# Seven quarter-size products in place of eight for half of a first layer, with float16 operands and partial sums seeded into PSUM by a copy

## The chip, the cores and the metric

The kernel runs on one core of a Trainium2 chip. The metric is device time in microseconds (us), as the median of several executions; the kernel before takes 293.1 us in the runs made for this study. A run more than 1.5% above the fastest of the same kernel counts as slow and is left out of the ratios. "Granted clock" is the share of full speed that the chip granted TensorE, as the trace records it.

## The reference

Sliding-window attention (window of 32 on each side, 8 heads of 64) is followed by two dense layers with a gelu between them:

```python
def _attn_ref(q, k, v):                       # q, k, v: (8, 8, 576, 64)
    scores = scale * np.matmul(q, k.transpose(0, 1, 3, 2))
    scores = np.where(np.abs(pos[:, None] - pos[None, :]) <= 32, scores, -1e9)
    ...                                       # softmax
    return np.matmul(attn, v)

def _moe_ref(x, w_in, w_out):                 # x: 4608 x 512, w_in: 512 x 2048, w_out: 2048 x 512
    h = x @ w_in
    g = h * (1.0 / (1.0 + np.exp(-1.702 * h)))
    return g @ w_out
```

## The kernel before

The 4608 rows are 36 *units* of 128 rows. The main loop goes by *windows* of two units (a and b, 256 rows). In window w the kernel computes attention of its own two units, the first layer of the pair before, and the second layer of the pair before that. The second layer already is a seven-product scheme (P1 to P7), whose operand sums VectorE makes (`g_sums`). The first layer is plain: eight groups of eight matmuls, each group followed by one gelu on ScalarE, in two PSUM banks by turns.

```python
    def two_banks(self, name, dtype=F32):
        return self.ps.tile([128, 2, 512 if dtype == F32 else 1024], dtype, name=name, tag="a", bufs=2)

    def layer1(self, t, d, kind="h"):
        ...
        hps = self.bank(kind, [128, 2, 256], F32, "h_ps")        # kind "h": two buffers
        ffs = (d, d + 8) if t > 2 else (2 * d, 2 * d + 1)
        for i in range(2):
            ff = ffs[i]
            for kr in range(self.NK):                            # NK = 4
                nc.tensor.matmul(hps[:, i, :], self.w_in_sb[:, kr, ff * 128:(ff + 1) * 128], self.xT[t][:, kr, :],
                                 start=(i == 0 and kr == 0), stop=(i == 1 and kr == self.NK - 1))
        nc.scalar.activation(self.g[t][:, ffs[0]:ffs[1] + 1:ffs[1] - ffs[0], :], hps, AF.Gelu_apprx_sigmoid)

    def window(self, w):                 # the steady part; t = w - 2; l1 holds the 8 groups of pair w - 1
        ...
        self.scores(a)
        self.scores(b)
        self.g_sums(t, 1, (0, 1))
        self.product(t, 1, "o")
        self.keep(t, 1, dve)
        self.product(t, 2, "h")
        self.g_sums(t, 1, (2, 3))
        ...                              # P5, softmax of a, P6, softmax of b
        run(l1)
        self.values(a)
        self.values(b)
        self.norm(a)
        self.x_T(a)
        self.product(t, 7)
        self.keep(t, 7, dve)
        self.result(t, 22)
        run(l1, 1)
        self.product(t, 4)
        self.result(t, 21, act)
        self.norm(b)
        self.x_T(b)
        self.product(t, 3)
        self.result(t, 12)
        run(l1, len(l1) - 4)
        self.g_sums(w - 1, 0)
        self.feed(w)                     # among other things four copies of v ("vo<-ve") on VectorE
        run(l1, 4)
```

The softmax here doesn't subtract the row's maximum and nothing guards it: scores larger than these inputs give would overflow.

Of the kernel before, what the change touches and what calls it, by code (L numbers as in the profile page):

```python
# [22 lines left out]
JT = 4  # L23
# [4 lines left out]
class _Kernel:  # L28
# [7 lines left out]
    def __init__(self, ctx, tc, q, k, v, w_in, w_out, out):  # L36
        self.tc, self.nc = tc, tc.nc
        self.q, self.k, self.v, self.w_in, self.w_out, self.out = q, k, v, w_in, w_out, out
        self.B, self.H, self.S, self.D = q.shape
        self.N = self.B * self.S  # L40
        self.DM = self.H * self.D
        self.DFF = w_in.shape[1]
        self.NK = self.DM // 128
        self.NFF = self.DFF // 128
        self.scale = 1.0 / (self.D ** 0.5)
        self.NU = self.N // 128
        self.NW = self.NU // 2

        def pool(name, bufs, **kw):
            return ctx.enter_context(tc.tile_pool(name=name, bufs=bufs, **kw))  # L50

        self.cst = pool("cst", 1)
        self.work = pool("work", 2)
        self.ps = pool("ps", 1, space=bass.MemoryType.PSUM)
        self.stage, self.paired = {}, set()
        self.span = {"A": (0, 320)}
        self.xT, self.g, self.o_ps = {}, {}, {}
        self.p, self.acc, self.x, self.sc = {}, {}, {}, {}
        self.gs, self.part, self.o_sb = {}, {}, {}

# [10 lines left out]
    def two_banks(self, name, dtype=F32):  # L71
        return self.ps.tile([128, 2, 512 if dtype == F32 else 1024], dtype, name=name, tag="a", bufs=2)


    def setup(self):
# [3 lines left out]
        self.w_in_sb = cst.tile([128, self.NK, self.DFF], BF16, name="w_in_sb")  # L79
# [141 lines left out]
    def load_raw(self, c, hp, eng):  # L221

        lo, size = self.tokens("A")
        raw = self.stage[c, "raw", hp] = self.cst.tile([size // JT, 2, JT * self.D], F32, name=f"{c}_raw{hp}")
        src = {"q": self.q, "k": self.k}[c]
        eng.dma_start(raw, src[0, 2 * hp:2 * hp + 2, lo:lo + size, :].rearrange("h (p j) d -> p h (j d)", j=JT))
# [30 lines left out]
    def score_banks(self):  # L257
        return self.two_banks("sc").rearrange("k e (h s) -> k e h s", s=SQ)
# [9 lines left out]
    def scores(self, u):  # L268
        nc = self.nc
        seen = u not in self.sc  # L270
        if seen:
            self.sc[u] = self.score_banks()
# [27 lines left out]
    def values(self, u, kinds=None):  # L300
        nc, D = self.nc, self.D
        p = self.p.pop(u)
        if kinds is None:
            both = self.two_banks("pv")[:, :, :4 * (D + 1)].rearrange("q i (h d) -> q i h d", d=D + 1)
# [11 lines left out]
    def norm(self, u):  # L316
        nc, D = self.nc, self.D
        acc = self.acc.pop(u)
        x = self.work.tile([128, self.H, D], BF16, name="x", tag="x", bufs=4)
# [14 lines left out]
    def x_T(self, u, kind=None, eng=None):  # L334
        nc = self.nc
        t, s = divmod(u, 2)
        if s == 0:
            self.xT[t] = self.work.tile([128, self.NK, 256], BF16, name="xT", tag="xT", bufs=4)
# [5 lines left out]
        tp = self.bank(kind, [128, 4, 128], BF16, "tp")  # L344
        for c in range(4):
            nc.tensor.transpose(tp[:, c, :], x[:, 2 * c:2 * c + 2, :], self.ident)  # L346
# [16 lines left out]
    def layer2(self, u, quarter, kind="o", eng=None):  # L363
# [9 lines left out]
        if quarter == 3:  # L373
            o_sb = self.work.tile([128, self.DM], F32, name="o_sb", tag="o_sb", bufs=4)
# [53 lines left out]
    def result(self, t, n, eng=None):  # L428
# [3 lines left out]
        if u not in self.o_sb:  # L432
            self.o_sb[u] = self.work.tile([128, self.DM], F32, name="o_sb", tag="o_sb", bufs=4)
# [33 lines left out]
    def head(self):  # L467
# [8 lines left out]
        self.setup_neg()  # L476
        for m in range(2):
            self.load_v(m)
# [138 lines left out]

    def window(self, w):
# [19 lines left out]
        if w == 4:  # L638
# [22 lines left out]
            loads()  # L661
            for m in (10, 11):
# [9 lines left out]
        self.scores(a)  # L672
        if w > 5:
            self.scores(b)
# [4 lines left out]
        if w == 5:  # L679
            self.scores(b)  # L680
# [9 lines left out]
        self.values(a)  # L690
        self.values(b)
# [4 lines left out]
        self.result(t, 22)  # L696
        run(l1, 1)
# [114 lines left out]
```

## Time and profile before

| what | before |
|---|---|
| time | 293.29 us (292.95 to 293.41, 3 runs); 293.12 in the rounds with the changed kernel |
| TensorE busy | 283.5 us, 97% of the span, granted clock 1.0 |
| VectorE, ScalarE, GpSimd busy | 62%, 62%, 35% |
| one window | 14.63 us, of which TensorE is busy 14.63 |

The lines behind this table, and how they are read, are in the prediction below. Two more are wanted later. The first is from the page's part on the chain that ended last (each engine's share of the chain of work that sets the end); the second is the page's row of the first sum of g (after the bar: busy us, mean ns of one; then the idle time before them).

```profile
PE 82%; DMA 12%; POOL 3%; DVE 1%; issue 1%; ACT 0%; POOLq 0%; DVEq 0%
...
L398 DVE TENSOR_TENSOR gs<-g 128x512 f16<-128x512 f16 x30 | 12.8, 425 | 38.3 <-ACT g L361 38.3
```

ScalarE has 0% of the chain and VectorE 1%. A sum of g takes 0.425 us. VectorE's idle time before these sums, 38.3 us, is spent waiting for gelus, and since VectorE is hardly on the chain, it costs next to nothing.

### The profile page before, as it was taken

Reading aid. Unit: us, or ns where it says so; the run is one execution under the profiler, and the core shown is the slowest. Engines: PE = TensorE matmul, PEld = TensorE weight load, DVE = VectorE, ACT = ScalarE, POOL = GpSimd, SP = SyncE. Lnnn points to the kernel's source line nnn. Section 1 sums busy time; section 2 is a strip of 40 time slices with the busy share of each in tenths; the row PEclk is TensorE's granted clock in tenths of the full one; section 3 lists DMA queues with packets and bytes.
Section 4 is the critical chain, followed back from the end, with each engine's and each line's share of the span. In section 5 each row is a group of like instructions: output and inputs, shape, how many; then the busy total and the mean of one; then the engine's idle time right before and its main releaser. Section 6 shows DMA issues by size and latency. Waiting matters only on the chain.

```text
span 291.9 us, 8879 instructions
## 1 busy us (share of the span) xinstructions
PE 283.5 (97%) x3759; PEld 234.3 (80%) x3759; DVE 181.9 (62%) x465; ACT 181.1 (62%) x265; POOL 102.2 (35%) x140
## 2 busy tenths in 40 slices
PE   7989998999999999999999999999999999999994
PEld 2668654866888888888888888888888888888883
DVE  6761556578566767676767675757575757573352
ACT  4576365695757676767676666666666666664330
POOL 8864424988536341642525343422000000000000
PEclk9999999999999999999999999999999999999999
DMA  9999998999999999999999999999925221212012
GB/s 150 188 199 205 198 184 136 171 132 133 187 138 173 147 190 140 176 135 159 160 188 107 168 122 141 146 149 138 166 42 146 39 90 20 93 20 90 2 72 73
DMA packets 144823, 38.78 MB, mean 133 GB/s; under 512 B 129936, under 2 KB 140432, under 8 KB 144784
## 3 DMA queue, kind: packets, MB, share of 16 engines
q0 software_dynamic: 97232, 18.16, 85.0%
q1 hardware_dynamic: 47104, 19.67, 39.3%
q8 instruction: 29, 0.48, 0.7%
q10 hardware_dynamic: 448, 0.39, 0.5%
q14 instruction: 10, 0.08, 0.1%
HBM read 36.96 MB, written 9.44 MB: 159 GB/s over the span
## 4 chain that ended last, share of the span: by engine, by line
PE 82%; DMA 12%; POOL 3%; DVE 1%; issue 1%; ACT 0%; POOLq 0%; DVEq 0%
PE h_ps L359 38%; PE o_ps L421 32%; DMA ks<-in_k_dram 5%; DMA ve<-in_v_dram 4%; PE pv L313 4%; PE o_ps L371 4%; PE sc L282 3%; DMA w_in_sb<-in_moe_w_in_dram 3%; POOL ve L168 1%; PE tp L187 1%; POOL ks L146 0%; POOL ks L206 0%; POOL qs L206 0%; PE tp L346 0%; DVE o_sb L439 0%
## 5 line engine op out<-in xcount | busy, mean ns | idle before, releaser
L359 PE MATMUL h_ps<-xT,w_in_sb 128*128 128x256 bf16 x1152 | 134.9, 273 | 0.0
L361 ACT ACTIVATE g<-h_ps 128x512 f16<-128x512 f32 x144 | 85.7, 596 | 75.8 <-PE h_ps L359 74.5
L359 PEld LDWEIGHTS <-w_in_sb 128*128 128x128 bf16 x1152 | 112.2, 98 | 13.4
L168 POOL DMA_DIRECT2D ve<-in_v_dram x41 | 34.4, 847 | 73.1 <-DVE rec L323 46.3
L421 PEld LDWEIGHTS <-gs 128*128 128x128 f16 x480 | 45.7, 98 | 6.0 <-issue 0.2
L421 PE MATMUL o_ps<-w_sum,gs 128*128 128x256 f16 x360 | 44.4, 273 | 0.0
L421 PEld LDWEIGHTS <-g 128*128 128x128 f16 x360 | 34.2, 98 | 4.5 <-ACT g L361 0.2
L288 ACT ACTIVATE p<-sc 128x1024 bf16<-128x1024 f32 x36 | 34.9, 1021 | 4.5 <-PE sc L282 4.4
L398 DVE TENSOR_TENSOR gs<-g 128x512 f16<-128x512 f16 x30 | 12.8, 425 | 38.3 <-ACT g L361 38.3
L114 DVE COPY part<-o_ps 128x256 f32<-128x256 f32 x45 | 19.1, 424 | 19.3 <-PE o_ps L421 18.2
L421 PE MATMUL o_ps<-w_out_sb,g 128*128 128x256 f16 x240 | 29.0, 273 | 0.0
L439 DVE TENSOR_TENSOR o_sb<-o_ps,part 128x256 f32<-128x256 f32 x45 | 19.0, 423 | 15.4 <-PE o_ps L421 14.7
L114 DVE COPY vo<-ve 64x528 bf16<-64x528 bf16 x71 | 23.8, 335 | 6.9 <-DMA ve<-in_v_dram 5.3
L156 POOL DMA_DIRECT2D qs<-in_q_dram x27 | 22.9, 869 | 7.2 <-DMA ks<-in_k_dram 6.0
L156 POOL DMA_DIRECT2D ks<-in_k_dram x27 | 22.8, 860 | 5.2 <-DMA ve<-in_v_dram 3.6
L324 DVE TENSOR_TENSOR x<-pv,rec 128x512 bf16<-128x512 f32 x33 | 22.8, 692 | 1.1
L371 PE MATMUL o_ps<-w_out_sb,g 128*128 128x512 f16 x96 | 23.2, 380 | 0.0
L298 DVE TENSOR_TENSOR p<-p,mask 128x1024 bf16<-128x1024 bf16 x32 | 21.8, 686 | 0.9 <-ACT p L288 0.7
L458 ACT ACT_TABLE_LOAD x15 | 19.2, 1283 | 0.3
L288 ACT ACT_TABLE_LOAD x15 | 19.2, 1283 | 0.3
L313 PEld LDWEIGHTS <-p 128*64 128x64 bf16 x576 | 11.7, 110 | 7.1 <-issue 3.4
L421 PE MATMUL o_ps<-w_out_sb,gs 128*128 128x256 f16 x120 | 15.6, 273 | 0.0
(81 smaller groups left out, 232.4 us busy)
## 6 DMA issues: line engine op xcount, KB each, us to landing
out_dram<-o_sb SPq DMA_DIRECT2D x34, 256.0 KB, 4.8
ve<-in_v_dram POOLq DMA_DIRECT2D x31, 128.0 KB, 6.0
ks<-in_k_dram POOLq DMA_DIRECT2D x24, 128.0 KB, 7.8
qs<-in_q_dram POOLq DMA_DIRECT2D x24, 128.0 KB, 9.9
w_in_sb<-in_moe_w_in_dram POOLq DMA_DIRECT2D x4, 512.0 KB, 8.8
w_out_sb<-in_moe_w_out_dram POOLq DMA_DIRECT2D x4, 512.0 KB, 14.1
ve<-in_v_dram POOLq DMA_DIRECT2D x10, 64.0 KB, 5.9
ks<-in_k_dram POOLq DMA_DIRECT2D x7, 64.0 KB, 5.6
```

The costliest lines, as they stand in the source:

```text
L114: (eng.copy if eng is self.nc.scalar else eng.tensor_copy)(out, in_)
L156: self.nc.gpsimd.dma_start(self.stage[key][off:off + m, n], src[b, :, s:s + m, :].rearrange("h s d -> s h d"))
L168: self.nc.gpsimd.dma_start(self.ve[m % NV][lo + off:lo + off + n, :, :self.D], self.v[b, :, s:s + n, :].rearrange("h s d -> s h d"))
L288: nc.scalar.activation(p, sc, AF.Exp, scale=self.scale)
L298: self.nc.vector.tensor_mul(pv, pv, msk.to_broadcast([128, 8, 2, SQ]))
L313: nc.tensor.matmul(acc[half][blk * 64:blk * 64 + 64, hh, :], p[:, h % 2, h // 2 * 2 + blk, :], vt[:, h, :D + 1], start=(hh == 0), stop=(hh ...
L324: nc.vector.tensor_mul(x.rearrange("q (i h) d -> q i h d", i=2), acc[0][:, :, :, :D], rec4.to_broadcast([128, 2, 4, D]))
L359: nc.tensor.matmul(hps[:, i, :], self.w_in_sb[:, kr, ff * 128:(ff + 1) * 128], self.xT[t][:, kr, :], start=(i == 0 and kr == 0), stop=(i = ...
L361: nc.scalar.activation(self.g[t][:, ffs[0]:ffs[1] + 1:ffs[1] - ffs[0], :], hps, AF.Gelu_apprx_sigmoid)
L371: nc.tensor.matmul(o_ps, self.g[t][:, ff, s * 128:(s + 1) * 128], self.w_out_sb[:, ff, :], start=(ff == 0), stop=(ff == self.NFF - 1))
L421: nc.tensor.matmul(self.part[t, key], x, y, start=(first and k == 0), stop=(k == 7), skip_group_check=True)
L458: self.nc.scalar.activation(self.spark, self.spark, AF.Gelu_apprx_sigmoid)
```

## The change

The intent is to save TensorE work. Half of the first layer's output (four of the eight groups) is computed as a 2 x 2 block product with seven quarter-size products in place of eight. This takes sums of blocks of x and of w_in (both on GpSimd), and sums of the products. Some of those sums are made in PSUM: a copy seeds an accumulator with a partial sum, and the next product accumulates on top of it. x and w_in become float16 (presumably so that the sums keep more digits; no run tests this). There are two accumulators, `main` and `side`, the two banks of one PSUM tile. I write S1 to S7 for the seven products `seven(.., n)`, and d0 to d3 for the four plain groups that stay. In the excerpt, `...` marks cuts, and the comments behind # are mine.

```diff
-    def two_banks(self, name, dtype=F32):
-        return self.ps.tile([...], dtype, name=name, tag="a", bufs=2)
+    def two_banks(self, name, dtype=F32, which=None):
+        if which is None:
+            which, self.turn = self.turn, 1 - self.turn
+        return self.ps.tile([...], dtype, name=name, tag=f"a{which}", bufs=1)
...
-        self.w_in_sb = cst.tile([128, self.NK, self.DFF], BF16, name="w_in_sb")
+        self.w_in_sb = cst.tile([128, self.NK, self.DFF], F16, name="w_in_sb")
+        self.wi_sum = cst.tile([128, 4, 2, self.DFF // 4], F16, name="wi_sum")
...
+    def w_in_sums(self):                                  # once, in window 4
+        w, ws, pool = self.w_in_sb, self.wi_sum, self.nc.gpsimd
+        pool.tensor_add(ws[:, 0], w[:, top, v], w[:, low, v])
+        pool.tensor_sub(ws[:, 1], ws[:, 0], w[:, top, u])
+        pool.tensor_sub(ws[:, 2], w[:, top, u], w[:, top, v])
+        pool.tensor_sub(ws[:, 3], w[:, low, u], ws[:, 1])
+    def x_sums(self, t):                                  # in every window from 6 on
+        xs = self.xs[t] = self.work.tile([128, 4, 2, 128], F16, name="xs", tag="xs", bufs=1)
+        ...                                               # four sums or differences on GpSimd
+    def seven(self, t, n):                                # eight matmuls of N=128 into main (n = 1, 6, 5, 3) or side
+        ...
+            both = self.two_banks("h_ps", which=1).rearrange("p i (f s) -> p i f s", f=4)
+            hs["main"], hs["side"] = both[:, 0], both[:, 1]
+        ...
+    def move(self, key, src, eng, add=None):              # copy, or addition on VectorE
+    def gelu(self, t, src, low, v):                       # gelu of one quarter
...
+            self.seven(w - 1, 1)
+            self.move("side", "main", dve)
+            self.values(b, which=0)
+            ...
+            run(l1, 1)
+            self.product(t, 4)
+            self.result(t, 21, act)
+            self.seven(w - 1, 2)
+            self.gelu(w - 1, "side", 0, 0)
+            self.seven(w - 1, 6)
+            self.move("k2", "main", act)
+            self.product(t, 3)
+            self.result(t, 12)
+            self.seven(w - 1, 7)
+            self.move("k7", "side", act)
+            self.seven(w - 1, 5)
+            self.move("22", "main", dve, "k7")
+            self.feed(w)
+            run(l1, 2)
+            self.gelu(w - 1, "22", 1, 1)
+            self.g_sums(w - 1, 0, (0, 1))
+            self.seven(w - 1, 4)
+            self.move("21", "side", dve, "k2")
+            self.gelu(w - 1, "21", 1, 0)
+            self.seven(w - 1, 3)
+            self.gelu(w - 1, "main", 0, 1)
+            self.g_sums(w - 1, 0, (2, 3))
+            return
```

More of the change, by code (lines that the diff above doesn't have):

```diff
@@ L59, in __init__ @@
         self.gs, self.part, self.o_sb = {}, {}, {}
+        self.xs, self.hs, self.turn = {}, {}, 0
     def bank(self, kind, shape, dtype, name):
@@ L69, in bank @@
         return self.ps.tile(shape, dtype, name=name, tag=kind, bufs={"h": 2, "o": 1, "t": 1}[kind])
-    def two_banks(self, name, dtype=F32):
-        return self.ps.tile([128, 2, 512 if dtype == F32 else 1024], dtype, name=name, tag="a", bufs=2)
+    def two_banks(self, name, dtype=F32, which=None):
+        if which is None:
+            which, self.turn = self.turn, 1 - self.turn
+        return self.ps.tile([128, 2, 512 if dtype == F32 else 1024], dtype, name=name, tag=f"a{which}", bufs=1)
     def setup(self):
@@ L78, in setup @@
         self.mask = cst.tile([128, 4, SQ], BF16, name="mask")
-        self.w_in_sb = cst.tile([128, self.NK, self.DFF], BF16, name="w_in_sb")
+        self.w_in_sb = cst.tile([128, self.NK, self.DFF], F16, name="w_in_sb")
+        self.wi_sum = cst.tile([128, 4, 2, self.DFF // 4], F16, name="wi_sum")
+        self.ident16 = cst.tile([128, 128], F16, name="ident16")
         self.w_out_sb = cst.tile([128, self.NFF, self.DM], F16, name="w_out_sb")
@@ L223, in load_raw @@
         lo, size = self.tokens("A")
-        raw = self.stage[c, "raw", hp] = self.cst.tile([size // JT, 2, JT * self.D], F32, name=f"{c}_raw{hp}")
+        if "raw" not in self.stage:
+            self.stage["raw"] = self.work.tile([128, 4, 2, JT * self.D], F32, name="raw", tag="gs")
+        raw = self.stage[c, "raw", hp] = self.stage["raw"][:size // JT, 2 * hp + "kq".index(c)]
         src = {"q": self.q, "k": self.k}[c]
@@ L255, in setup_neg, with score_banks @@
                               op0=ALU.mult, op1=ALU.add)
-    def score_banks(self):
-        return self.two_banks("sc").rearrange("k e (h s) -> k e h s", s=SQ)
+    def score_banks(self, which=None):
+        return self.two_banks("sc", which=which).rearrange("k e (h s) -> k e h s", s=SQ)
     def blind(self, u):
@@ L266, in blind, with scores @@
                                   start=True, stop=False, skip_group_check=True)
-    def scores(self, u):
+    def scores(self, u, which=None):
         nc = self.nc
@@ L271, in scores @@
         if seen:
-            self.sc[u] = self.score_banks()
+            self.sc[u] = self.score_banks(which)
         sc = self.sc.pop(u)
@@ L298, in band, with values @@
         self.nc.vector.tensor_mul(pv, pv, msk.to_broadcast([128, 8, 2, SQ]))
-    def values(self, u, kinds=None):
+    def values(self, u, kinds=None, which=None):
         nc, D = self.nc, self.D
@@ L303, in values @@
         if kinds is None:
-            both = self.two_banks("pv")[:, :, :4 * (D + 1)].rearrange("q i (h d) -> q i h d", d=D + 1)
+            both = self.two_banks("pv", which=which)[:, :, :4 * (D + 1)].rearrange("q i (h d) -> q i h d", d=D + 1)
             acc, self.acc[u] = [both[:, i] for i in range(2)], [both]
@@ L318, in norm @@
         acc = self.acc.pop(u)
-        x = self.work.tile([128, self.H, D], BF16, name="x", tag="x", bufs=4)
+        x = self.work.tile([128, self.H, D], F16, name="x", tag="x", bufs=4)
         rec = self.work.tile([128, self.H, 1], F32, name="rec", tag="rec", bufs=3)
@@ L337, in x_T @@
         if s == 0:
-            self.xT[t] = self.work.tile([128, self.NK, 256], BF16, name="xT", tag="xT", bufs=4)
+            self.xT[t] = self.work.tile([128, self.NK, 256], F16, name="xT", tag="xT", bufs=4)
         x = self.x.pop(u)
@@ L343, in x_T @@
             return
-        tp = self.bank(kind, [128, 4, 128], BF16, "tp")
+        tp = self.bank(kind, [128, 4, 128], F16, "tp")
         for c in range(4):
-            nc.tensor.transpose(tp[:, c, :], x[:, 2 * c:2 * c + 2, :], self.ident)
+            nc.tensor.transpose(tp[:, c, :], x[:, 2 * c:2 * c + 2, :], self.ident16)
         self.cast(eng or nc.vector, out, tp)
@@ L373, in layer2 @@
         if quarter == 3:
-            o_sb = self.work.tile([128, self.DM], F32, name="o_sb", tag="o_sb", bufs=4)
+            o_sb = self.work.tile([128, self.DM], F32, name="o_sb", tag="o_sb", bufs=3)
             self.cast(eng or nc.vector, o_sb, o_ps)
@@ L432, in result @@
         if u not in self.o_sb:
-            self.o_sb[u] = self.work.tile([128, self.DM], F32, name="o_sb", tag="o_sb", bufs=4)
+            self.o_sb[u] = self.work.tile([128, self.DM], F32, name="o_sb", tag="o_sb", bufs=3)
         cols = slice(256 * half, 256 * half + 256)
@@ L476, in head @@
         self.setup_neg()
+        dve.tensor_copy(self.ident16, self.ident)
         for m in range(2):
@@ L616, in head @@
             self.rows_X(c, 3, (0, 1))
+    def w_in_sums(self):
+        w, ws, pool = self.w_in_sb, self.wi_sum, self.nc.gpsimd
+        top, low, u, v = slice(0, 2), slice(2, 4), slice(512, 1024), slice(1536, 2048)
+        pool.tensor_add(ws[:, 0], w[:, top, v], w[:, low, v])
[3 more added lines that the diff above has]
+    def x_sums(self, t):
+        pool, x = self.nc.gpsimd, self.xT[t]
+        xs = self.xs[t] = self.work.tile([128, 4, 2, 128], F16, name="xs", tag="xs", bufs=1)
+        top, low, u, v = slice(0, 2), slice(2, 4), slice(0, 128), slice(128, 256)
+        pool.tensor_sub(xs[:, 0], x[:, top, v], x[:, top, u])
+        pool.tensor_sub(xs[:, 1], x[:, low, v], xs[:, 0])
+        pool.tensor_sub(xs[:, 2], x[:, low, v], x[:, top, v])
+        pool.tensor_sub(xs[:, 3], x[:, low, u], xs[:, 1])
@@ new lines, in seven @@
+    def seven(self, t, n):
+        hs = self.hs
+        if n == 1:
+            both = self.two_banks("h_ps", which=1).rearrange("p i (f s) -> p i f s", f=4)
+            hs["main"], hs["side"] = both[:, 0], both[:, 1]
+        x, xs, w, ws = self.xT[t], self.xs[t], self.w_in_sb, self.wi_sum
+        dst = hs["main" if n in (1, 6, 5, 3) else "side"]
+        u, v = slice(0, 128), slice(128, 256)
+        for f in range(4):
+            here = slice(128 * f, 128 * f + 128)
+            top, low = slice(512 + 128 * f, 640 + 128 * f), slice(1536 + 128 * f, 1664 + 128 * f)
+            for k in range(2):
+                a, b = {1: (w[:, k, top], x[:, k, u]), 2: (w[:, 2 + k, top], x[:, 2 + k, u]),
+                        3: (ws[:, 3, k, here], x[:, 2 + k, v]), 4: (w[:, 2 + k, low], xs[:, 3, k]),
+                        5: (ws[:, 0, k, here], xs[:, 0, k]), 6: (ws[:, 1, k, here], xs[:, 1, k]),
+                        7: (ws[:, 2, k, here], xs[:, 2, k])}[n]
+                self.nc.tensor.matmul(dst[:, f], a, b, start=(n in (1, 7) and f == 0 and k == 0),
+                                      stop=(f == 3 and k == 1), skip_group_check=True)
@@ new lines, in move @@
+    def move(self, key, src, eng, add=None):
+        if key != "side":
+            self.hs[key] = self.work.tile([128, 2, 4, 128], F32, name="hs", tag="kc" if key[0] == "k" else "qc")[:, 0]
+        if add is None:
+            self.cast(eng, self.hs[key], self.hs[src])
+        else:
+            self.nc.vector.tensor_add(self.hs[key], self.hs[src], self.hs[add])
+    def gelu(self, t, src, low, v):
+        at = 12 if low else 4
+        self.nc.scalar.activation(self.g[t][:, at:at + 4, 128 * v:128 * v + 128], self.hs[src], AF.Gelu_apprx_sigmoid)
@@ L661, in window @@
             loads()
+            self.w_in_sums()
             for m in (10, 11):
@@ L671, in window @@
             return
-        self.scores(a)
         if w > 5:
-            self.scores(b)
+            self.x_sums(w - 1)
+        self.scores(a, which=0)
+        if w > 5:
+            self.scores(b, which=1)
         self.g_sums(t, 1, (0, 1))
@@ L679, in window @@
         if w == 5:
-            self.scores(b)
+            self.scores(b, which=1)
         self.g_sums(t, 1, (2, 3))
@@ L689, in window @@
         run(l1)
-        self.values(a)
-        self.values(b)
+        self.values(a, which=0)
+        if w == 5:
+            self.values(b, which=1)
         self.norm(a)
@@ L696, in window @@
         self.result(t, 22)
+        if w > 5:
+            self.seven(w - 1, 1)
+            self.move("side", "main", dve)
+            self.values(b, which=0)
+            self.norm(b)
+            self.x_T(b)
+            run(l1, 1)
[22 more added lines that the diff above has]
+            return
         run(l1, 1)
```

## The prediction

> **What bounds the kernel now.** I read the page's engine shares first, then the chain of work that ended last, then busy time by stretch, then the timeline of one window. The page gives the shares and the groups that matter (after the bar: busy us, mean ns of one; idle before).
>
> ```profile
> PE 283.5 (97%) x3759; PEld 234.3 (80%) x3759; DVE 181.9 (62%) x465; ACT 181.1 (62%) x265; POOL 102.2 (35%) x140
> L359 PE MATMUL h_ps<-xT,w_in_sb 128*128 128x256 bf16 x1152 | 134.9, 273 | 0.0
> L361 ACT ACTIVATE g<-h_ps 128x512 f16<-128x512 f32 x144 | 85.7, 596 | 75.8 <-PE h_ps L359 74.5
> L324 DVE TENSOR_TENSOR x<-pv,rec 128x512 bf16<-128x512 f32 x33 | 22.8, 692 | 1.1
> ```
>
> TensorE has no gaps; ScalarE (ACT) waits for it. The chain, restricted to 85 to 275 us, is TensorE alone:
>
> ```profile
> by line: PE h_ps L359 48.8%; PE o_ps L421 42.8%; PE pv L313 4.3%; PE sc L282 4.1%
> ```
>
> The changed code runs in windows 6 to 17, each one pair of 128-row units. In the timeline their scores start every 14.63 us, from 92.48 to 253.62 us. One window in the view of busy time by stretch:
>
> ```profile
> core 0: us, PE busy (x) PEld busy (x) DVE busy (x) ACT busy (x) POOL busy (x), PEclk, DMA share, GB/s
> 209.73:224.36 14.63, 14.63 (x201) 12.82 (x200) 9.56 (x25) 9.74 (x14) 0.00 (x0) 1.00 0.42 100
> ```
>
> So a window lasts exactly as long as TensorE's stream, at full clock. Anything added to TensorE's stream, or any wait put into it, is paid in full, twelve times.
>
> The timeline shows why the waits are hidden and gives the handover times I use below (start us, duration us):
>
> ```profile
> 219.03 5.40 PE L359 MATMUL h_ps<-xT,w_in_sb 128*128 128x256 bf16 x48
> ...
> 220.98 0.60 ACT L361 ACTIVATE g<-h_ps 128x512 f16<-128x512 f32 x1 [0.28 <-PE h_ps L359]
> ...
> 221.61 0.43 DVE L398 TENSOR_TENSOR gs<-g 128x512 f16<-128x512 f16 x1 [1.95 <-ACT g L361]
> ...
> 222.07 0.42 DVE L400 TENSOR_TENSOR gs<-gs,g 128x512 f16<-128x512 f16 x1
> 222.41 0.42 DVE L402 TENSOR_TENSOR gs<-g 128x512 f16<-128x512 f16 x1
> ```
>
> Six groups of eight matmuls alternate between two PSUM banks, so a gelu reads one while TensorE fills the other. Handovers: 48 matmuls in 5.40 us are (5.40-0.273)/47 = 0.109 us apart. A group's stream ends 0.109 us after its last start, that matmul ends 0.164 us later, the gelu starts 0.03 us after that: 0.20 us from stream end to gelu. Gelu end (221.58) to VectorE (DVE) start (221.61): 0.03. A dependent sum follows after 0.46, an independent operation 0.34 later. VectorE to TensorE is about 0.06 (in the head, an x ends at 19.45 and its transpose starts at 19.51).
>
> [...] The trace has such pairs:
>
> ```profile
> 59.87 0.39 PE L187 MATMUL tp<-ident,qc 128*128 128x128 bf16 x4
> ```
>
> Four transposes, each with its own weights; one lasts 0.219 us, so they are (0.39-0.219)/3 = 0.057 us apart. [...]
>
> ```profile
> 47.96 2.81 POOL L114 COPY kc<-ks 128x512 bf16<-128x512 bf16 x4 [8.13 <-DMA ks<-in_k_dram]
> 50.72 2.29 POOL L114 COPY qc<-qs 128x512 bf16<-128x512 bf16 x4
> ...
> 49.61 0.68 DVE L298 TENSOR_TENSOR p<-p,mask 128x1024 bf16<-128x1024 bf16 x1
> ```
>
> Equal copies, but the first four took 0.52 us more, and a VectorE product with two SBUF inputs runs just there.
>
> **The change part by part.** Write S1 to S7 for the seven products, d0 to d3 for the four groups that stay, "main" and "side" for the two accumulator banks.
>
> *Stream.* Removed per window: 4 groups of 8 matmuls at N=256, 32 x 0.109 = 3.49 us. Added: 7 x 8 at N=128, 56 x 0.056 = 3.14 us. Saved: 0.35. The second unit's values now stand apart from the first's; each visit to that shape costs TensorE a 0.21 us gap (waits view):
>
> ```profile
> PEld L313 <- issue: 2.5, 12, 0.2
> ```
>
> Net -0.15 us per window, -1.8 us over twelve. Float16 changes nothing: existing float16 matmuls take the same 273 ns.
>
> *Engine loads.* VectorE gains three 128x512 PSUM operations, 3 x 0.69 = 2.1 us on 9.6; ScalarE two copies, about 0.59 each (the row of 128x512 copies out of PSUM) on 9.74, its gelus staying the same size. Both fit in a window. It is not load that matters but order.
>
> *New waits of TensorE.* I read the built program's order and resolved each semaphore wait to the instruction that satisfies it. Both accumulators are slices of one tile, and a write to either waits for the last reader of either:
> - S6 (main) waits for the gelu that reads side after S2, which directly precedes it: 0.20 + 0.60 + 0.06 = 0.86 us.
> - S5 (main) waits for the copy of side after S7, which directly precedes it: 0.20 + 0.59 + 0.06 = 0.85.
> - S3 (main) waits for the addition that reads side after S4. VectorE runs in order, and ahead of that addition stand two g sums that need the gelu of d3, the group before S4. From the stream end of d3: 0.20 + gelu 0.60 + 0.03 + first sum 0.46 + second 0.34 + addition 0.69 + 0.06 = 2.38; S4 covers 0.45. Stall 1.93.
> - The next window's second scores use the same two banks, and wait for the gelu after S3: 0.20 + 0.60 + 0.05 less the first scores' 0.32: 0.5.
>
> S2 (waits for the copy main to side), S7 and S4 are covered by 1.75 us or 0.87 us of other matmuls. Second values wait for the first normalisation, about 1.2 us after the first values; P7 and S1, 1.3 us, just cover it.
>
> *GpSimd.* Four x sums per window start when S4 ends (their one buffer), at 0.7 us after d3. [...] They meet exactly the two g sums of the third stall, which start at 0.83. If each sum must wait for one of them, the addition moves from 1.63 to about 2.97: up to 1.35 us more in eleven windows. I count 65%. The weights' sums, once, are about 9 us of GpSimd in window 4, far ahead of their first use: nothing.
>
> *Sum.* -1.8 + 12 x (0.86 + 0.85 + 1.93) = 43.7, + 11 x 0.5 = 5.5, + 0.65 x 11 x 1.35 = 9.7: +57.1. 293.3 + 57 = 350 us; the period goes from 14.63 to about 19.5 us.
>
> **Rivals.** (1) The intended gain: if the waits were by bank, or hidden, -1.8 us or, with the values still free, -4: 289 to 292. For it: the arithmetic of seven for eight and the agreeing 0.057. Against it: the waits stand in the program, and three producers directly precede their waiters. (2) [...] For it: the trace shows only GpSimd held up by VectorE, not the reverse. [...] (4) GpSimd late with x sums or loads: it idles about 5 us per window in the middle of the run, and S6 needs its sums some 13 us after S4; no effect. (5) Gaps of about 3 us let the clock drop: [...] but it lengthens the upper tail.
>
> **Range and chances.** All handovers come from rows of this trace, so the main uncertainty is contention (340 against 354) and a few tenths per stall, each times twelve. 350 us, 8 in 10 between 336 and 362. Faster by over 2%: 0.03, only if I resolved the waits wrongly; within 2%: 0.04; slower by over 2%: 0.93.
>
> **What would show it.** The score starts should be about 19 to 20 us apart; TensorE idle about 4 to 5.5 us per window, with S6 and S5 each waiting 0.8 to 0.9 us for ScalarE, S3 2 to 3.3 us for VectorE, the second scores 0.5 us for ScalarE; S matmuls 0.056 us apart; the g sums beside x sums longer than 0.42 us, or starting late. A period below 15 us, or S3 starting straight after S4, would prove me wrong.

## The result

The changed kernel is correct and takes 364.18 us (363.58 to 366.76, 4 runs, all in the fast state), against 293.12 (292.71 to 293.41) for the kernel before on the same chip: a ratio of 1.244, 95% interval 1.238 to 1.251. Ratios here are those on record, from the fast runs of both kernels, so not quite the ratio of the medians. The direction was as predicted; the size was not. The prediction said 350 us with a range to 362, and the measurement lies 14 us above the middle and 2 us outside the range.

The page of the changed kernel: shares of the engines, the granted clock in 40 slices, the chain, and the row of the first sum of g.

```profile
PE 305.2 (84%) x4045; PEld 246.5 (68%) x4047; DVE 226.4 (63%) x502; ACT 196.1 (54%) x289; POOL 145.8 (40%) x192
...
PEclk9899999998999998989898998989898998989999
...
PE 75%; DVE 12%; ACT 8%; issue 2%; DMA 2%; POOL 0%; POOLq 0%; ACTq 0%; DVEq 0%
...
L405 DVE TENSOR_TENSOR gs<-g 128x512 f16<-128x512 f16 x30 | 17.6, 585 | 11.7 <-ACT g L368 7.0
```

TensorE is now idle 16% of the time, and VectorE and ScalarE have come onto the chain with 12% and 8%. A matmul of the plain groups in float16 takes 274 ns, where the row of before had 273 in bfloat16, so the type costs nothing. The sum of g takes 0.585 us on average, no longer 0.425. And the clock row has eights in it, at regular distances: the mean granted clock is 0.943, where it was 1.0.

The view of waits names what TensorE waited for (us in total, times, longest):

```profile
PE h_ps L662 <- DVE hs L672: 29.8, 12, 2.6
PE h_ps L662 <- ACT g L677: 8.5, 12, 0.8
PE h_ps L662 <- ACT hs L119: 8.1, 12, 0.7
PE sc L289 <- DVE qT L849: 1.9, 1, 1.9
```

These are three of the four waits that the prediction named (S3 for the addition on VectorE, S6 for a gelu, S5 for a copy), twelve times each, and one that it did not name: the scores of window 5 waited 1.9 us once. The fourth, of the second scores for the gelu after S3, stands in this view only once (0.3 us); with the clock at full it comes back (e1_fill below).

From one start of scores to the next, windows 6 and 7 take 18.97 and 19.37 us. Windows 8 to 16 take 20.54 to 20.60 each, and window 5, which has no seven products at all, takes 18.40 where it took 14.86.

### Where the third wait comes from

The timeline of the changed kernel around S3 (start us, duration us, engine; in brackets the idle time before it and what ended it):

```profile
193.18 0.66 POOL L640 TENSOR_TENSOR xs<-xT 128x256 f16<-128x256 f16 x1 [2.90 <-PE h_ps L662]
193.26 0.87 DVE L405 TENSOR_TENSOR gs<-g 128x512 f16<-128x512 f16 x1
193.92 0.73 POOL L641 TENSOR_TENSOR xs<-xT,xs 128x256 f16<-128x256 f16 x1
194.16 0.77 DVE L407 TENSOR_TENSOR gs<-gs,g 128x512 f16<-128x512 f16 x1
194.86 0.68 DVE L672 TENSOR_TENSOR hs<-h_ps,hs 128x512 f32<-128x512 f32 x1
195.59 0.75 PE L662 MATMUL h_ps<-xT,wi_sum 128*128 128x128 f16 x8 [2.55 <-DVE hs L672]
196.27 1.40 PE L289 MATMUL sc<-qT,kT 64*64 64x128 bf16 x48
197.60 2.75 PE L428 MATMUL o_ps<-w_out_sb,g 128*128 128x256 f16 x16
```

GpSimd's sums of x start when S4 has ended and run beside VectorE's two sums of g, which take 0.87 and 0.77 us in place of 0.43 and 0.42. The addition that S3 waits for starts behind them. The gap is 2.55 us. After it comes something unexpected: the 48 matmuls of the scores take 1.40 us, where the kernel before has 0.70 for them, and P1 with P2 takes 2.75, where window 5 of the same trace has 1.92.

### What happens after the gap

Raw records of the granted clock in this trace change only on a fixed grid with steps of 3.413 us. I cut the trace on that grid and asked for busy time by stretch. The three pairs are: the gap before S3 in window 6 and the step after it; the same in window 7; the wait of the scores in window 5 and the step after it.

```profile
core 0: us, PE busy (x) PEld busy (x) DVE busy (x) ACT busy (x) POOL busy (x), PEclk, DMA share, GB/s
110.57:113.98 3.41, 1.46 (x18) 1.25 (x16) 2.93 (x8) 1.71 (x3) 1.73 (x3) 1.00 1.87 172
113.98:117.40 3.42, 2.51 (x67) 2.14 (x67) 2.63 (x6) 2.78 (x4) 1.10 (x2) 1.00 1.18 123
131.05:134.47 3.42, 0.87 (x15) 0.66 (x12) 3.05 (x5) 1.60 (x3) 2.83 (x4) 1.00 1.60 169
134.47:137.88 3.41, 3.29 (x60) 2.51 (x59) 1.59 (x5) 3.35 (x5) 0.00 (x0) 0.50 0.72 93
79.85:83.27 3.42, 1.53 (x35) 1.30 (x34) 3.38 (x10) 1.79 (x2) 3.42 (x4) 1.00 1.53 112
83.27:86.68 3.41, 3.41 (x19) 2.15 (x17) 2.36 (x6) 1.66 (x3) 2.67 (x4) 0.50 2.80 143
```

In window 6 the gap of 2.55 us is cut by the grid, 1.96 us of idle time fall into one step, and the clock stays at 1.00. In window 7 the whole gap falls into one step, TensorE is busy only 0.87 us of it, and the whole next step is granted half speed. In window 5, 1.89 us of idle time in one step were enough. So a step need not be without any work for half speed to follow; here TensorE worked for 25% and 45% of it. The two steps with 1.96 and 1.89 us of idle time also show that idle time alone does not decide. From window 7 to window 16 every gap falls wholly into one step: a window with the half-speed step lasts 20.58 us, and six steps are 20.48, so the gap hardly moves on the grid. I had not expected that lock. (In window 17 the gap has moved far enough: 1.76 us of it fall into one step, and full speed follows.)

### What happened in window 5

The timeline around the start of window 5 (its scores start at 77.62 us before and at 77.75 in the changed kernel), first the kernel before, then the changed one:

```profile
70.54 1.91 DVE L114 COPY vo<-ve 64x528 bf16<-64x528 bf16 x4
```

```profile
70.67 7.71 DVE L119 COPY vo<-ve 64x528 bf16<-64x528 bf16 x4
...
71.76 2.13 POOL L630 TENSOR_TENSOR wi_sum<-w_in_sb 128x1024 f16<-128x1024 f16 x1
...
78.19 2.50 POOL L633 TENSOR_TENSOR wi_sum<-w_in_sb,wi_sum 128x1024 f16<-128x1024 f16 x1
...
78.75 2.23 DVE L407 TENSOR_TENSOR gs<-gs,g 128x512 f16<-128x512 f16 x1
...
81.94 0.45 PE L289 MATMUL sc<-qT,kT 64*64 64x128 bf16 x24 [1.89 <-DVE qT L849]
```

While GpSimd sums the weights (four instructions of 2.12 to 2.50 us, 8.9 us in all), VectorE's four copies take 7.71 us, not 1.91, and a sum of g takes 2.23 us. VectorE is then late with a copy that the scores need. "Far ahead of their first use" was true of the sums themselves, and it was the wrong question.

### The profile page after: what moved, and what is told of

Same layout as the page of the kernel before. It is cut to its first block, busy times and chain, and to the rows that moved or that the text cites. A ratio compares the mean times of both kernels' runs of the same rounds, so it can differ in the third digit from the quotient of the medians.

```text
span 361.9 us, 9602 instructions
## 1 busy us (share of the span) xinstructions
PE 305.2 (84%) x4045; PEld 246.5 (68%) x4047; DVE 226.4 (63%) x502; ACT 196.1 (54%) x289; POOL 145.8 (40%) x192
## 4 chain that ended last, share of the span: by engine, by line
PE 75%; DVE 12%; ACT 8%; issue 2%; DMA 2%; POOL 0%; POOLq 0%; ACTq 0%; DVEq 0%
PE o_ps L428 27%; PE h_ps L366 21%; PE h_ps L662 11%; PE o_ps L378 5%; ACT g L677 4%; PE pv L320 3%; PE sc L289 3%; DVE gs L407 3%; DVE gs L405 3%; DVE vo L119 2%; DVE hs L672 2%; ACT hs L119 2%; ACT g L368 2%; DMA qs<-in_q_dram 2%; PE tp L192 1%
## 5 line engine op out<-in xcount | busy, mean ns | idle before, releaser
L368 ACT ACTIVATE g<-h_ps 128x512 f16<-128x512 f32 x96 | 57.2, 597 | 87.3 <-PE h_ps L366 87.3
L366 PE MATMUL h_ps<-xT,w_in_sb 128*128 128x256 f16 x768 | 94.0, 274 | 0.0
L366 PEld LDWEIGHTS <-w_in_sb 128*128 128x128 f16 x768 | 73.6, 98 | 9.4
L662 PEld LDWEIGHTS <-wi_sum 128*128 128x128 f16 x384 | 24.4, 101 | 53.0 <-issue 41.8
L662 PE MATMUL h_ps<-xs,wi_sum 128*128 128x128 f16 x288 | 22.1, 219 | 16.7 <-ACT g L677 8.5
L662 PE MATMUL h_ps<-xT,wi_sum 128*128 128x128 f16 x96 | 9.4, 256 | 29.8 <-DVE hs L672 29.8
L672 DVE TENSOR_TENSOR hs<-h_ps,hs 128x512 f32<-128x512 f32 x24 | 16.4, 684 | 17.2 <-PE h_ps L662 17.2
L677 ACT ACTIVATE g<-hs 128x512 f16<-128x512 f32 x24 | 15.0, 627 | 21.1 <-DVE hs L672 21.1
L119 ACT COPY hs<-h_ps 128x512 f32<-128x512 f32 x24 | 14.1, 586 | 17.9 <-PE h_ps L662 17.9
L331 DVE TENSOR_TENSOR x<-pv,rec 128x512 f16<-128x512 f32 x33 | 22.8, 691 | 1.1
```

What stands on the lines that cost most here:

```text
L119: (eng.copy if eng is self.nc.scalar else eng.tensor_copy)(out, in_)
L331: nc.vector.tensor_mul(x.rearrange("q (i h) d -> q i h d", i=2), acc[0][:, :, :, :D], rec4.to_broadcast([128, 2, 4, D]))
L662: self.nc.tensor.matmul(dst[:, f], a, b, start=(n in (1, 7) and f == 0 and k == 0), stop=(f == 3 and k == 1), skip_group_check=True)
L672: self.nc.vector.tensor_add(self.hs[key], self.hs[src], self.hs[add])
L677: self.nc.scalar.activation(self.g[t][:, at:at + 4, 128 * v:128 * v + 128], self.hs[src], AF.Gelu_apprx_sigmoid)
```

## The experiments

Ten kernels ran, each beside the kernel before on the same chip; the record has no others. The run with eight products and the two of the last call were timed in five rounds, the others in three (e5b_spread_dve was put down for five, but has only as many times as those with three). Medians of the kernel before in the three calls were 293.43, 292.97 and 293.38 us. All results are correct, but for one run that is wrong on purpose.

### e1_fill: idle matmuls in the gap

Eleven matmuls that nobody reads, N=512, into a PSUM bank that is dead at that time, keep TensorE busy while S3 waits.

```diff
             self.gelu(w - 1, "21", 1, 0)
+            self.keep_busy(11, "t")
             self.seven(w - 1, 3)
```

> Eleven idle matmuls of 512 columns (0.216 us each, 2.4 us) stand between product 4 and product 3, in a bank that is dead there; they fill the gap of 2.55 us in which TensorE waits for VectorE and delay nothing. Theory A (the part of the time that my sum left out is the half clock that follows the gap, ten times 3.4 us of it): the clock stays at full, the period falls from 20.58 to about 19.4 us, time about 352 us. Rival B (the half clock costs little, because the work in it waits anyway, and the excess is elsewhere): still 360 to 365 us.

In the timeline of e7_split_fill, which has the same fill, the eleven take 2.54 us; one matmul of 512 columns takes 0.38 (the row of the kernel before), so they are (2.54 - 0.38)/10 = 0.216 us apart.

It took 350.42 us (349.58 to 351.71), granted clock 1.0, a ratio of 1.194 (1.188 to 1.199). More work for TensorE made the kernel 13.8 us faster. The wait that is left, in the view of waits:

```profile
PE h_ps L662 <- DVE hs L672: 1.9, 11, 0.2
```

The period is 19.37 us in every window from 7 on. The half clock therefore costs 13.8 us. The traces say the same: ten windows of 20.58 in place of 19.37 are 12.1 us, and window 5 with 18.40 in place of this run's 16.87 is 1.5. Only the 12.1 are the work of the added matmuls: in window 5 nothing was filled, but here the grid happened to cut its gap (at most 1.29 us of idle time in one step). The view also has the fourth wait of the prediction, of the second scores for the gelu after S3: 3.4 us in eleven times.

### e2_add_first: the addition ahead of the sums of g

```diff
-            self.g_sums(w - 1, 0, (0, 1))
             self.seven(w - 1, 4)
             self.move("21", "side", dve, "k2")
+            self.g_sums(w - 1, 0, (0, 1))
```

> The addition that product 3 waits for goes ahead of the two g sums on VectorE. Theory A (in-order VectorE is what makes product 3 wait, 2.7 us in the stream, and the gap lets the clock drop): the wait shrinks to about 0.95 us (0.20 + 0.69 + 0.06), the clock stays at full: 364 - 12 x 1.75 - 12 = about 331 us. Rival B (the g sums themselves set the end, in the next window): the wait moves to a product that needs them and the time falls by less than 10 us.

It took 329.99 us (329.44 to 330.42), clock 1.0, ratio 1.123; the period is 17.61 us.

```profile
PE h_ps L662 <- DVE hs L672: 9.6, 12, 0.9
```

The third wait falls from 2.6 to at most 0.9 us, and with it goes the half clock; 331 us had been expected. This confirms that most of the third wait was the order on VectorE, not TensorE or the addition itself. Against the filled kernel it is 1.76 us a window, 20.4 us in all.

### e3_xs2: two buffers for the sums of x

With a second buffer the sums need not wait for S4, and should run before the sums of g. To have room, the softmax buffer goes from 5 to 4.

```diff
-        p = self.work.tile([128, 2, 8, SQ], BF16, name="p", tag="p", bufs=5)
+        p = self.work.tile([128, 2, 8, SQ], BF16, name="p", tag="p", bufs=4)
...
-        xs = ... name="xs", tag="xs", bufs=1)
+        xs = ... name="xs", tag="xs", bufs=2)
```

Theory A here and in e6_one_xsum is that the sums of g are long only because they run beside the sums of x. By the timeline of the changed kernel that comes to about 0.80 us a window, (0.87 - 0.43) + (0.77 - 0.42).

> Two buffers for the x sums (paid for by one p buffer fewer), so that GpSimd need not start them when product 4 ends, where they meet the g sums. Theory A [...]: g sums back at 0.42 us, product 3's wait down from 2.55 to about 1.75 us; if the clock then no longer drops, about 343 us, if it does, about 355 us. Rival B (the longer g sums come from something else, such as the float16 x): g sums stay at 0.77 to 0.87 us and the time within 1%.

It took 362.59 us (358.77 to 365.53), ratio 1.230, clock about 0.95 in its runs; its profile fell in the slow state. The page has, for the first sum of x:

```profile
L640 POOL TENSOR_TENSOR xs<-xT 128x256 f16<-128x256 f16 x12 | 8.7, 721 | 75.1 <-DMA xT<-x 75.1
```

The sums now wait for the transposed x (a DMA), not for S4. In that profile they meet VectorE's copies of v in part, the gap is 1.8 to 3.2 us, and the clock still drops. By its time alone, within 1% of 364 us, the run would speak for the rival; but it is inconclusive on what the contention costs, because the sums only met other work and the clock hides the rest. The next call therefore measured it without the clock.

### e4_split: a group between S7 and S5

```diff
             self.move("k7", "side", act)
+            run(l1, 1)
             self.seven(w - 1, 5)
...
-            run(l1, 2)
+            run(l1, 1)
```

> One of the two groups that stay is moved between product 7 and product 5, so that the copy of the side bank is read beside it. Theory A (each wait in the stream is paid in full unless other matmuls stand in it): the wait of product 5, 0.84 us per window, goes, about 354 us with the half clock still there. Rival B (the chain through VectorE and ScalarE is the bound, not TensorE's stream): the wait turns up at product 4 or 3 and the time stays within 1% of 364 us.

It took 360.79 us (360.25 to 363.98), ratio 1.231, clock 0.947: 3.4 us gained, a third of the 10 that I expected, and within the 1% that the rival had put down. The wait of S5 for the copy is gone from the view of waits, but the third has grown to as much as 3.0 us. The group that covers S5 was taken from before S4, where it had covered VectorE's work. Again the clock disturbs the comparison: the raw records have eleven half-speed steps, each 20.48 us after the last, and the windows 7 to 16 take 20.47 us on average, where the same order takes 18.91 at full clock (e7_split_fill below). So here too the period stays at six steps of the clock's grid. That this took up part of the gain is my reading; no run separates it.

### e6_one_xsum: no sums of x in the loop (wrong on purpose)

The sums of x are made once and then reused, so all later results are wrong, but the schedule loses just GpSimd's part. The gap is filled, with seven idle matmuls as it gets shorter.

```diff
         pool, x = self.nc.gpsimd, self.xT[t]
+        if t > 5:
+            self.xs[t] = self.xs[5]
+            return
...
+            self.keep_busy(7, "t")
             self.seven(w - 1, 3)
```

> Wrong result on purpose: the x sums are made once and used in all windows, so GpSimd sums nothing beside the g sums; seven idle matmuls (1.5 us) keep the clock up in the shorter gap. To be held against the run with the gap filled (350.4 us, period 19.37). Theory A [...]: g sums at 0.42 us, period about 18.57, time about 341.6 us. Rival B (something else makes the g sums long): they stay at 0.77 to 0.87 us, time about 350 us.

It took 341.18 us (340.24 to 345.33), period 18.55 us, and was wrong as intended (relative error 0.90). The first sum of g is back to its old duration:

```profile
L405 DVE TENSOR_TENSOR gs<-g 128x512 f16<-128x512 f16 x30 | 12.7, 424 | 15.1 <-ACT g L680 7.9 <-ACT g L368 7.0
```

Against e1_fill, 19.37 less 18.55 is 0.82 us a window, 9.2 us in all. That is what the sums of x cost beside the sums of g.

### e7_split_fill: the split with the gap filled

The edits of e4_split and e1_fill together.

> The split (a staying group between products 7 and 5) together with the filled gap. Theory A (the wait of product 5 is 0.84 us of pure loss; without the fill its gain was partly lost to the clock and to a longer wait before product 3): 350.4 - 12 x 0.84 = about 340 us. Rival B (what product 5 no longer waits, product 3 waits, since the chain through VectorE and GpSimd sets the end): 345 to 351 us, with a longer wait before product 3.

It took 347.22 us (345.14 to 348.35), period 18.91: a gain of 0.46 us a window over e1_fill, not the 0.84 of the S5 wait that it removes, and so what the rival expected. The view of waits has S3 waiting for the addition for 5.1 us in twelve times, where e1_fill has 1.9. In its timeline the copies of v, which follow the addition after S5, run until 223.68 us, and the first sum of g starts at 223.60, though its gelu had ended at 222.75. With only one group left between S5 and S4, VectorE is still at the copies when the gelu is ready. Half of the wait moved to S3, so the waits can't be removed one by one: the cover for one is taken from the next.

### e8_eight: all of the change but the seven products

The float16 types, the two fixed PSUM tiles and the sums of the weights stay; the loop computes all eight plain groups as before.

```diff
-        if w > 5:
-            self.x_sums(w - 1)
...
-        if w == 5:
-            self.values(b, which=1)
+        self.values(b, which=1)
...
-        if w > 5:
+        if w > 99:
             self.seven(w - 1, 1)
```

> Everything of the change but the seven products and the x sums: float16, the four weight sums on GpSimd in window 4, the fixed bank pairs, the smaller buffers; eight products as before. Theory A (the weight sums lock VectorE's copies out for 2.0 us in window 5, the rest costs nothing): 295 us, window 5 at 16.9 us, the others at 14.63. Rival B (my prediction's 'nothing'): 293 us.

It took 295.69 us (295.06 to 298.32), ratio 1.011 (1.007 to 1.014). Window 5 takes 16.98 us, not 14.86, and most others 14.63. So float16, the new PSUM tiles and the smaller buffers cost nothing that shows in the loop, and window 5 loses about 2 us. The cause is the sums of the weights on GpSimd, by the copies above (7.71 us for 1.91; 5.88 in this run's timeline) and by the next run: it makes these sums on VectorE, behind the copies, and has window 5 back at 14.86 us.

### e5b_spread_dve: a better order

Here every S product has at least one full product or group between itself and the next: values(a), S1, P7, values(b), S2, P4, S6, d, S7, P3, S5, d, S4, d, S3. The addition goes ahead of the sums of g, the second scores come after P1, and VectorE makes the sums of the weights.

```diff
-        w, ws, pool = self.w_in_sb, self.wi_sum, self.nc.gpsimd
+        w, ws, pool = self.w_in_sb, self.wi_sum, self.nc.vector
...
             self.seven(w - 1, 2)
             self.gelu(w - 1, "side", 0, 0)
+            self.product(t, 4)
+            self.result(t, 21, act)
             self.seven(w - 1, 6)
             self.move("k2", "main", act)
+            run(l1, 1)
+            self.seven(w - 1, 7)
+            self.move("k7", "side", act)
             self.product(t, 3)
             self.result(t, 12)
-            self.seven(w - 1, 7)
-            self.move("k7", "side", act)
             self.seven(w - 1, 5)
...
```

> Seven products kept, but each reader of the two banks gets other matmuls to run beside it: product 1 right after the first values, then one full product or staying group between every two of the seven; the addition ahead of the g sums; the next window's second scores after its first product; weight sums on VectorE. Theory A (order alone made the loss; nothing in seven products is slow): waits of 0.1 us or so each, period about 14.9 us, clock at full, 291 to 298 us. Rival B (the longer VectorE and ScalarE chain cannot be hidden in a 14.6 us window): period above 16 us, over 310 us.

It took 309.26 us (308.89 to 309.62), ratio 1.055, clock 1.0: far better than the changed kernel, and a miss against the 291 to 298 that I expected, close to the rival's 310. Window 6 takes 14.75 us, the others 15.8 to 16.8. The timeline of a later window has

```profile
204.19 0.67 POOL L640 TENSOR_TENSOR xs<-xT 128x256 f16<-128x256 f16 x1 [1.96 <-DMA xT<-x]
204.33 2.79 DVE L119 COPY vo<-ve 64x528 bf16<-64x528 bf16 x4
```

and the view of waits begins with a wait that the other kernels don't have:

```profile
PE o_ps L428 <- DVE gs L405: 6.6, 9, 1.1
```

GpSimd's sums now meet the copies of v, which take 2.79 us, and then the products of the second layer wait for sums of g that VectorE makes late. The contention had only moved.

### e9_late_xsums: the sums of x held back

GpSimd first copies one column of the second softmax, so that its sums start after it, in a stretch in which VectorE mostly reads PSUM. In the timeline of this run the four sums take 0.67 us each, and a normalisation and a copy out of PSUM that VectorE makes beside them take 0.69 us each, no more than without sums beside them (0.69 in the rows of the kernel before).

```diff
         self.band(b)
+        if w > 5:
+            self.nc.gpsimd.tensor_copy(self.hold, self.p[b][:, 0, 0, 0:1])
+            self.x_sums(w - 1)
```

> The kernel of the spread order, but the sums of x are held back until the second softmax's product with the mask is done (a copy of one column makes GpSimd wait for it), so that they should meet only normalisations and copies out of PSUM on VectorE, and no longer the copies of v (SBUF to SBUF) or the sums of g. Theory: the spread order lost its last 16 us to GpSimd's sums of x meeting VectorE's copies. Then the period falls from 15.8 to 16.8 us to the 14.75 of window 6 (at most 14.95), the time to 294 to 297 us, and the four copies of v take about 1.3 us again, not 2.8. Rival, that the spread order itself starves P1 and P5 of their sums of g, whatever GpSimd does: the period stays over 15.5 us and the time over 303 us. If GpSimd's sums come too late for the fourth product (they now end some 4 us later in the window), a new wait of that product on GpSimd shows instead.

It took 296.32 us (295.14 to 297.71), ratio 1.010 (1.007 to 1.013), with a period of 14.92. The four copies in its timeline:

```profile
211.74 1.23 DVE L120 COPY vo<-ve 64x528 bf16<-64x528 bf16 x4
```

The 13 us between this run and e5b_spread_dve (each held against its own runs of before) are the contention; the spread order did not starve P1 and P5 by itself.

### e10_both_scores: both scores behind P1

```diff
-        self.scores(a, which=0)
-        if w == 6:
-            self.scores(b, which=1)
         self.product(t, 1, "o")
-        if w > 6:
+        if w > 5:
+            self.scores(a, which=0)
             self.scores(b, which=1)
```

> As the run with late sums of x, but both units' scores stand together behind P1, which saves one change into and out of the 64-row shape, about 0.19 us a window. If these changes of shape cost what the gaps in the spread order's trace say (0.094 and 0.095 us), the period is 14.56 to 14.8 us and the time 291 to 295 us, 2 us below the run with late sums. If the later scores make the softmax late instead, the second values or the first normalisation wait on VectorE and nothing is gained. In no case is more than 1% gained over the kernel before: eight products' stream less 0.35 us, plus one visit for the split values (0.19) and two handovers still open (0.145 and 0.143).

It took 295.51 us (294.62 to 296.63), ratio 1.007 (1.004 to 1.010). That is slightly above the 291 to 295 that I expected. One window in the view of busy time by stretch, between two starts of scores:

```profile
212.44:227.25 14.81, 14.81 (x227) 12.49 (x226) 10.97 (x28) 10.54 (x17) 2.76 (x5) 1.00 0.46 92
```

The period is 0.11 us below that of the run before it, not 0.19, and 0.18 above the 14.63 of the kernel before; the times of the two runs overlap. TensorE is busy throughout as the profile counts it, but modelled ends hide gaps of a tenth of a microsecond. Two handovers are left, and the separate visit of values(b). In the timeline d2 starts at 208.59 us and S4 at 209.60, d3 at 210.06 and S3 at 211.01; a group's stream takes 8 x 0.109 = 0.87, so the gaps are about 0.14 and 0.08 us, the second smaller than the 0.143 that I had put down. If both were hidden too, 14.81 less 0.22 would be 14.59. That is 0.04 us a window below the kernel before, about 0.5 us in twelve, an estimate from these numbers that no run has shown. None of the versions I ran beats the kernel before.

## Why the prediction was right or wrong

**The bound and the direction: right.** TensorE's stream set the window, and each wait in it was paid in full, twelve times.

**The stream: right.** S matmuls, each with its own weights, are 0.056 us apart in the trace, which is the figure in the prediction's 56 x 0.056. Eight of them last 0.61 us, one of them 0.219, and (0.61 - 0.219)/7 is 0.056. Longer streams at N=128 were not run.

**The first two waits: right.** The timeline of the changed kernel shows S2's gelu, then S6, and S5 behind its copy:

```profile
207.48 0.60 ACT L677 ACTIVATE g<-h_ps 128x512 f16<-128x512 f32 x1
...
208.13 0.62 PE L662 MATMUL h_ps<-xs,wi_sum 128*128 128x128 f16 x8 [0.69 <-ACT g L677]
...
210.78 0.61 PE L662 MATMUL h_ps<-xs,wi_sum 128*128 128x128 f16 x8 [0.67 <-ACT hs L119]
```

Idle time counts from the end of the last matmul, about 0.16 us after the stream could have gone on; so 0.69 and 0.67 idle are 0.85 and 0.84 us in the stream, where I had worked out 0.86 and 0.85. The fourth wait, put down as 0.5, is right too: e1_fill has 0.31 us idle a window for it, and a matmul of the scores lasts 0.19 us where the stream goes on after 0.01.

**The third wait and the contention: right, the contention smaller.** I had put down 1.93 us, and up to 1.35 more if each sum of g has to wait for a sum of x, at 65%; rival (2), with 340 us, had nothing more. The 1.35 was my estimate, and no trace of the kernel before shows the length of a sum of x. With the first two as the changed kernel's trace has them, 0.66 and 0.73 us, the same sum is 1.23: 0.70 + 0.66 + 0.43 + 0.73 + 0.34 less 1.63. The sums overlap only in part (0.87 and 0.77 us beside them, not 0.43 and 0.42), and e6_one_xsum measures 0.82 us. The expected value that I had counted, 0.65 times 1.35, is 0.88. That the two agree is luck: I had weighed all against nothing, and it was neither.

**The sum at full clock: right.** 14.63 - 0.15 + 0.86 + 0.85 + 1.93 + 0.5 + 0.82 is 19.44 us a window; e1_fill, which has the same waits but a full clock, has 19.37, and a time of 350.42 us against my 350. (In the prediction's sum, 43.7 is the product alone, without the -1.8 before it; the total of 57.1 is right.) The time is that close partly by luck, as the point on the weights' sums shows.

**The clock: wrong, and this is the step that failed.** Rival (5) says that gaps of about 3 us let the clock drop, and I charged it to the upper tail alone. I took my gap to be just too short for that; this was my assumption, and no trace of the kernel before shows it. The trace of the changed kernel shows half speed after steps with 2.55 us of idle time and once after 1.89, full speed once after 1.96, and e1_fill shows that this costs 13.8 us. 350 and 13.8 is 364 us, the time measured. The prediction saw the danger, had a gap of 2 to 3.3 us in hand, and gave it no weight in the middle and too little in the range.

**The weights' sums: wrong, but small.** "Far ahead of their first use: nothing" asks only when the result is needed. The change costs about 2 us here: e8_eight shows 16.98 us for window 5 in place of 14.86. The prediction had seen the two engines meet in the trace (four GpSimd copies in 2.81 us, not 2.29, beside a VectorE product) and counted such a meeting for the sums of x only. It does not show in the total: the twelve windows of e1_fill (4.74 us each over before, 0.4 less in the first) and its window 5 make about 58.5 us, and the measured difference is 57.0. By the two profiles' score starts, e1_fill reaches window 5 0.95 us earlier than the kernel before, and from the start of window 17 to the end it takes 3.5 us more, not 4.74. So about 2 us were gained outside these windows and hide the 2 us of window 5; why, no run shows.

**What stays open.** The exact rule of the clock. In the trace of the changed kernel, steps of the loop with 1.76 and 1.96 us of idle time were not followed by half speed, and those with 1.89 and with 2.54 or more were; in its head, among short transposes, even a step with 1.02 was. So idle time alone is not what is counted. The ends of matmuls are modelled, and no run here varies the gap by itself. Open too is the obvious other way out, the prediction's rival (1). `main` and `side` are slices of one tile, and the traces show the waits of S6 and S5 end with a reader of the *other* slice (S6 starts 0.05 us after the gelu that reads `side`). S3's wait is of the same kind: the addition before it reads `side`. No run gave each accumulator a tile of its own, so whether these three waits would go without a new order is not shown.

## What to carry to other kernels

When TensorE has no gaps, count a change in handovers before counting it in matmuls: this one saved 0.35 us of stream a window (32 x 0.109 less 56 x 0.056, the spacings in the traces) and put four waits of 0.5 to 2.7 us into it, and even the best order that I ran stayed 0.18 us a window above the kernel before. A product that must wait for another engine's read of the same tile, here 0.85 us, needs about a full group of other matmuls (0.87 us) between them, and that cover can be spent only once. A gap need not fill a clock step of 3.4 us: in the trace of the changed kernel every step of the loop with 2.54 us or more of idle time (ten of them) was followed by half speed, and one of two just under 2 us was (1.89, not 1.96), so such a gap should be charged the half-speed step too; and anything put on GpSimd should be checked against what VectorE does *at that time*, however early its result is ready: beside GpSimd's sums here four copies on VectorE took 7.71 us in place of 1.91, and two sums of g 0.87 and 0.77 in place of 0.43 and 0.42.
